# Another order for the list of work in a clustered-attention and SiLU kernel, with some V loads on another queue

## The chip, the cores and the metric

The kernel runs on one core of a Trainium2 chip. Its time is the time of one execution on the device in microseconds (us); lower is better. The program is one launch, and its outputs are float32.

## The reference

Clustered attention is followed by a two-layer block. There are 4 batches, 8 heads, 768 rows, head size 64 and 16 centroids for each head; a query sees only the keys that fall to the same centroid as it does.

```python
q_n, k_n, c_n = (each divided by its norm + 1e-06)
q_assign = argmax(einsum('bhsd,hcd->bhsc', q_n, c_n))      # the same for k
mask = q_assign[:, :, :, None] == k_assign[:, :, None, :]
scores = where(mask, q @ k^T / sqrt(64), -1e9)
attn = exp(scores - max); attn = attn / (sum(attn) + 1e-09)
x = (attn @ v)  -> [3072 tokens, 512]
h = x @ w_in                                               # 512 x 2048
out = (h / (1 + exp(-h))) @ w_out                          # 2048 x 512
```

## The kernel before, in words

The attention has 32 heads ("jobs" 0 to 31, of batches 0 to 3), and each job is 6 scores tiles and 6 exponentials. The block behind it works on a batch in two halves of 384 tokens. Everything on the chip is issued from one string, `order`, a list of 1796 words. A loop at the end takes word after word, splits it at its points and calls the function of that name, so a word's place in the list is the place of its instructions in the in-order queue of every engine that they go to. Buffers and banks are handed out in the same order. The first number of a word is the job or the batch; a last letter names the engine (A ScalarE, D VectorE, P GpSimd, S SyncE), and what follows @ names the bank.

```python
    for word in order:
        word, _, n = word.partition("@")
        name, *rest = word.split(".")
        words[name](tuple(rest), [int(y) for y in n] or None)
    ...
    def load_v(i, eng=nc.sync):
        vn = mp.tile([128, NJ, D], f32, name="vn", bufs=5)
        eng.dma_start(vn.rearrange("p j d -> p (j d)"), v[i // H, i % H].rearrange("(p j) d -> p (j d)", j=NJ))
        vns[i] = vn
```

The words that the rest speaks of, with their lines in the profile:

- `ld.25` loads the queries and keys of job 25 as raw float32 (L108, two DMA issues on SyncE). `hi` (L120 on ScalarE, L124 on VectorE) and `lo` (L129) split them into two float16 parts, and `tp` (L138) transposes these by a DMA on SyncE.
- `L`, `ls`, `mx`, `ge` (L176, L188, L204, L213) work out which centroid each row belongs to. `sc` (L220 and L221, GpSimd) scales the codes; `cx` (L229, a transposing DMA on SyncE, cdt<-od) turns them; `mv` (L233, a DMA, ab<-cdt) puts them beside the transposed keys.
- `v.28.S` loads one job's V, 192 KB, from SyncE; with P at its end it loads it from GpSimd (L289). `vc` casts it on GpSimd (L294).
- `s` (L353) is two of a job's scores matmuls, and `x` (L358) the exponential on ScalarE. `pv` (L370) is the product with V, `nm` (L380, L382) the division by the sum, on VectorE.
- `xd` (L409, xt<-xn) transposes two heads' normalised result by a DMA on SyncE. The tile `xt` of one half of a batch is whole when four of them have landed: `xd.8.1`, `xd.10.1`, `xd.12.1` and `xd.14.1` for the second half of batch 1.
- `q` (L547) are the seven block products of a Quad, by which x @ w_in is done with seven products of half size in place of eight; `tt` (L507) are the sums of blocks of `xt` that they take, on VectorE. Product 1 starts a bank named qa, 6 and 7 add to that bank; product 2 starts qb; product 5 starts qg and 3 adds to it. `qc` copies a bank before it goes on being added to (L557 on ScalarE, L559 on VectorE), `qa` (L564) adds, `qt` (L571) is the tanh, `qg` (L584) the gate. So product 7 of a Quad, which adds to bank qa, can't start until the copy `qc` number 2 has read that bank. Plain units of the same layer are `au`, `t`, `g` (L418, L438, L441).
- `pp`, `p1`, `pa`, `pu`, `pc`, ... (L683 to L718) are the same seven-product scheme for the second layer (`pc` is L708, on VectorE); `b`, `be`, `bs` are plain parts of it (L596, L602 or L604, and the store L609). `tw` (L629) and `un` (L495) are sums of weights, on VectorE.
- `np` is the place where the banks change from pairs to single ones, some 40 us ahead of the end.

Of the kernel before, what the change touches and what calls it, by code (L numbers as in the profile page):

```python
# [34 lines left out]
def kernel(  # L35
# [771 lines left out]
    def stk_ev(pst1):  # L807
# [25 lines left out]
        qa.0.0.1.1 qt.0.0.0.1 s.34 au.0.0.12@2 qg.0.0.0.1 q.0.0.1.6 od.1 qt.0.0.1.0 un.4.1 q.0.0.1.5@3 v.9.S s.32
        qg.0.0.1.0 qc.0.0.1.2.A qa.0.0.0.2 qc.0.0.1.5.A vc.10 q.0.0.1.7 qa.0.0.1.2 q.0.0.1.3 qa.0.0.1.3 x.32 q.0.0.0.4
        qt.0.0.0.3 qg.0.0.0.3 s.31 q.0.0.1.4 t.0.0.12 g.0.0.12 qt.0.0.1.3 qg.0.0.1.3 au.0.0.13@3 lo.8 tp.8 hi.9.D
        hi.10.A t.0.0.13 pv.0.1@1 qt.0.0.1.1 g.0.0.13 b.0.0.0.0@2 b.0.0.0.1 hi.11.A lo.11 x.31 x.34 nm.0.1 qg.0.0.1.1
        tp.11 qt.0.0.0.2 au.0.0.14@0 s.39 x.39 s.35 x.35 b.0.0.0.2 t.0.0.14 g.0.0.14 lo.9 s.37 x.37 v.15.S au.0.0.15@3
        t.0.0.15 tp.9 b.0.0.1.0@1 vc.9 s.38 x.38 s.33 x.33 qt.0.0.1.2 b.0.0.1.1 ld.13 g.0.0.15 lo.10 qg.0.0.0.2 s.45
        x.45 L.8.32@3 ls.8 hi.12.A mx.8 qg.0.0.1.2 s.40 x.40 b.0.0.0.3 be.0.0.0.D lo.12 pv.2.1@3 s.42 x.42 L.11.32@2
        nm.2.1 ls.11 tp.10 ld.14 s.41 b.0.0.1.2 s.36 x.41 s.47 x.47 ge.8 cd.8@2 ce.8.D cg.8 x.36 L.9.32@0 b.0.0.1.3  # L840
        s.46 be.0.0.1.A xp.0.1@2 pv.4.1@3 vc.15 tp.12 od.2 ls.9 mx.9 xe.0.1.A xp.2.1@0 ge.9 v.8.S s.44 hi.13.D lo.13
        x.46 s.43 mx.11 cd.9@2 ce.9.D nm.4.1 xe.2.1.A cg.9 L.10.32@1 b.0.0.2.0@0 b.0.0.2.1 v.11.S ls.10 hi.14.D x.44
# [267 lines left out]
```

## Time and profile before

| what | value |
|---|---|
| time, median of 3 runs | 297.5 us (297.18 to 299.89) |
| the profiled execution | 298.51 us, of which the span of instructions is 296.6 us |
| granted TensorE clock, mean | 0.993 |
| TensorE busy | 285.2 us, 96% of the span |
| VectorE busy | 262.2 us, 88% |
| ScalarE busy | 247.6 us, 83% |
| GpSimd busy | 61.9 us, 21% |

In the rows below PE is TensorE, PEld its loading of weights, DVE VectorE, ACT ScalarE, POOL GpSimd, SP SyncE; SPq and POOLq are the issues of DMAs by these two. A row of a timeline has start, duration, engine, line, operation, what is written and read, and the number of instructions in it; what stands in brackets at its end is how long the engine had waited and for what. A row of a table of windows has the stretch, its length, the busy time of each engine in it with the number of instructions, the granted clock, the DMA share and GB/s.

### The profile page before, as it was taken

The page shows a single profiled execution, that of the slowest core. Times are in us where ns is not written, and L with a number is a line of the kernel's source. Part 1 is how long each engine was busy: PE and PEld are TensorE (multiplying, and loading weights), DVE is VectorE, ACT ScalarE, POOL GpSimd, SP SyncE. Part 2 cuts the span into 40 slices and gives each one's busy share as a digit, 9 for nine tenths or more (in the row PEclk, how much of TensorE's full clock was granted, in tenths as well). Part 3 has the DMA queues.
Part 4 walks back from the last instruction along what each step waited for, and adds up shares of the span by engine and source line. Part 5 has one row for each costly group of instructions (what it writes and reads, how often), then busy time and mean ns, then how long its engine had stood idle before and what let it go on. Part 6 is the DMA issues. An engine that isn't in the chain of part 4 may idle for free.

```text
span 296.6 us, 8938 instructions
## 1 busy us (share of the span) xinstructions
PE 285.2 (96%) x3561; PEld 223.5 (75%) x3561; DVE 262.2 (88%) x578; ACT 247.6 (83%) x431; POOL 61.9 (21%) x116
## 2 busy tenths in 40 slices
PE   7899999999999999999699999999999999899995
PEld 3777757576866668778487887887888889799984
DVE  5998699899999999998889999999998888699863
ACT  5999999986998799999589998789999867947541
POOL 2499310121004122235231031253100000000000
PEclk9999999999999999999899999999999999999999
DMA  6978999997989869998689999654212202201023
GB/s 213 295 208 134 192 222 293 186 188 186 236 204 203 219 163 212 190 165 199 152 212 239 155 276 157 92 132 97 67 27 65 86 0 86 86 2 35 3 105 111
DMA packets 80554, 45.21 MB, mean 152 GB/s; under 512 B 58368, under 2 KB 77120, under 8 KB 80512
## 3 DMA queue, kind: packets, MB, share of 16 engines
q1 hardware_dynamic: 76080, 38.39, 57.2%
q0 software_dynamic: 4000, 5.82, 10.9%
q8 instruction: 28, 0.46, 0.6%
q10 hardware_dynamic: 432, 0.43, 0.4%
q14 instruction: 14, 0.11, 0.1%
HBM read 27.30 MB, written 6.29 MB: 113 GB/s over the span
## 4 chain that ended last, share of the span: by engine, by line
PE 49%; DVE 5%; DMA 1%; issue 1%; ACT 0%; SPq 0%; DVEq 0%
PE po L683 17%; PE pS L353 9%; PE qa L547 7%; PE pO L370 6%; PE ph L418 4%; PE qg L547 3%; PE qb L547 2%; DMA raw<-in_k_dram 1%; PE psN L176 1%; DVE hl L129 1%; DVE gt L584 1%; DVE gt L441 1%; DVE mxn L204 1%; DVE od L213 0%; DVE L L188 0%
## 5 line engine op out<-in xcount | busy, mean ns | idle before, releaser
L358 ACT ACTIVATE P<-pS 128x768 f16<-128x768 f32 x192 | 150.7, 821 | 12.6 <-PE pS L353 9.6
L353 PE MATMUL pS<-ab 128*128 128x384 f16 x384 | 88.3, 326 | 0.3 <-ACT P L358 0.3
L353 PEld LDWEIGHTS <-ab 128*128 128x128 f16 x384 | 33.7, 98 | 11.8 <-issue 1.0
L370 PEld LDWEIGHTS <-P 128*128 128x128 f16 x1152 | 39.8, 97 | 3.4 <-DVE ab L278 0.3
L370 PE MATMUL pO<-vt,P 128*128 128x65 f16 x1152 | 41.5, 193 | 0.2 <-DVE ab L278 0.2
L294 POOL CAST vt<-vn 128x384 f16<-128x384 f32 x32 | 20.8, 661 | 75.8 <-DMA vn<-in_v_dram 64.0
L683 PEld LDWEIGHTS <-gt 128*128 128x128 f16 x328 | 32.2, 99 | 5.8 <-issue 0.6
L547 PEld LDWEIGHTS <-ws 128*128 128x128 f16 x352 | 30.4, 98 | 8.0 <-issue 2.4
L418 PE MATMUL ph<-xt,win_s 128*128 128x384 f16 x160 | 32.2, 326 | 0.3 <-DVE cc L564 0.3
L129 DVE SCALAR_TENSOR_TENSOR hl<-raw,hl 128x768 f16<-128x768 f32 (+3 forms) x35 | 31.4, 902 | 0.9 <-ACT hl L120 0.7
L683 PE MATMUL po<-wout_s,gt 128*128 128x256 f16 x216 | 28.2, 278 | 0.5 <-DVE ot L708 0.5
L571 ACT ACTIVATE tn<-cc 128x384 f32<-128x384 f32 x48 | 24.9, 530 | 4.1 <-DVE cc L564 3.8
L584 DVE SCALAR_TENSOR_TENSOR gt<-tn,cc 128x384 f16<-128x384 f32 x48 | 26.8, 565 | 0.9 <-ACT tn L571 0.8
L547 PEld LDWEIGHTS <-win_s 128*128 128x128 f16 x264 | 23.3, 99 | 5.4 <-issue 1.7
L596 PE MATMUL po<-wout_s,gt 128*128 128x512 f16 x96 | 24.1, 379 | 0.1
L441 DVE SCALAR_TENSOR_TENSOR gt<-tn,ph 128x384 f16<-128x384 f32 x40 | 21.6, 548 | 1.8 <-ACT tn L438 1.7
L418 PEld LDWEIGHTS <-win_s 128*128 128x128 f16 x160 | 15.2, 97 | 9.4 <-issue 0.6
L438 ACT ACTIVATE tn<-ph 128x384 f32<-128x384 f32 x40 | 20.0, 522 | 1.6 <-PE ph L418 0.8
L547 PE MATMUL qa<-tt,ws 128*128 128x192 f16 x176 | 21.1, 249 | 0.0
L176 PEld LDWEIGHTS <-ab 128*128 128x128 f16 x458 | 16.8, 97 | 3.9 <-DVE ab L163 0.6
L382 DVE TENSOR_TENSOR xn<-pO,zr 128x384 f16<-128x384 f32 x32 | 17.8, 558 | 1.1
L176 PE MATMUL psN<-stk,ab 128*128 128x32 f16 (+1 forms) x458 | 18.5, 188 | 0.1
(126 smaller groups left out, 476.0 us busy)
## 6 DMA issues: line engine op xcount, KB each, us to landing
raw<-in_k_dram SPq DMA_DIRECT2D x31, 192.0 KB, 3.6
out_dram<-ot SPq DMA_DIRECT2D x23, 256.0 KB, 2.6
vn<-in_v_dram SPq DMA_DIRECT2D x27, 192.0 KB, 4.0
raw<-in_q_dram SPq DMA_DIRECT2D x24, 192.0 KB, 3.6
win_s<-in_moe_w_in_dram POOLq DMA_DIRECT2D x8, 256.0 KB, 6.6
wout_s<-in_moe_w_out_dram POOLq DMA_DIRECT2D x4, 512.0 KB, 13.6
cp<-gt SPq DMA_DIRECT2D x4, 256.0 KB, 3.9
vn<-in_v_dram POOLq DMA_DIRECT2D x5, 192.0 KB, 3.5
```

The source lines that it names most:

```text
L129: nc.vector.scalar_tensor_tensor(out=hl[:, s, 1, :], in0=raws[job.name][:, s, :], scalar=QS, in1=hl[:, s, 0, :], op0=ALU.mult, op1=ALU.sub ...
L176: nc.tensor.matmul(L[:, n % g, :, n // g], ab[:, i, :], stk[:, job.groups[i // 3][0], x : x + w], start=(x == 0), stop=(x + w == 2 * HC),)
L353: nc.tensor.matmul(pS[:, e, 0:HALF], abs_[kj.name][:, kn, :], rhs, start=True, stop=True)
L358: nc.scalar.activation(out=P, in_=pst.pop(u)[:, :, 0:HALF], func=AF.Exp, bias=0.0, scale=ESC)
L370: nc.tensor.matmul(o[:, (2 * t + h) * VW : (2 * t + h + 1) * VW], Ps[i + h, c, j // 2][:, j % 2, ts(t, 128)], vtb[(i + h) % 13][:, j, 0:VW ...
L418: nc.tensor.matmul(ph[:, 0:HALF], win_s[:, r, ts(fb, 128)], xts[b, c][:, r, :], start=(r == 0), stop=(r == NR - 1))
L441: nc.vector.scalar_tensor_tensor(out=gt[:, fb, :], in0=tn, scalar=1.0, in1=ph[:, 0:HALF], op0=ALU.add, op1=ALU.mult)
L547: nc.tensor.matmul(o[:, g * QT : (g + 1) * QT], w, y, start=(k in (1, 2, 5) and g == 0 and r == 0), stop=(r == 1), skip_group_check=True,)
L571: nc.scalar.activation(out=t, in_=self.src(n), func=AF.Tanh, bias=0.0, scale=1.0)
L584: eng.scalar_tensor_tensor(out=self.gt[:, f : f + 2, h], in0=self.tn[n].rearrange("p (g n) -> p g n", g=2), scalar=1.0, in1=self.src(n).re ...
L596: nc.tensor.matmul(po, gts[b, c][:, fc, ts(t, 128)], wout_s[:, fc, :], start=(fc == 0), stop=(fc == NFB - 1))
L683: nc.tensor.matmul(o, l[:, f, :], x, start=(f == 0 and k in begins), stop=(f == HK - 1), skip_group_check=True)
```

## The change

Only the string `order` changes. The first 245 words, the opening up to about 39 us of the profile, stay. The other 1551 words come in another order. They are the same words but for a few engine letters:

- V loads: `v.9`, `v.12`, `v.14`, `v.19`, `v.20`, `v.23`, `v.24` and `v.31` go from SyncE's queue to GpSimd's, `v.25` and `v.30` the other way (GpSimd issues 11 in place of 5, SyncE 21 in place of 27).
- `mv.17`, `mv.18`, `mv.21`, `mv.26` go from GpSimd's queue to SyncE's.
- The copies `be.0.0.0` and `be.0.1.0` go from VectorE to ScalarE; `hi.10`, `hi.12`, `hi.19` from ScalarE to VectorE; `hi.17`, `hi.27` from VectorE to ScalarE; some 14 of the `qc` copies change between the two, nearly as many each way (ScalarE has 38 in place of 39).

Of the list itself, the first changed line and the one that takes its place:

```diff
-        ld.10 qc.0.0.0.1.A ld.9 s.30 t.0.0.6 q.0.0.0.2@3 s.29 ld.12 ae.0.0.7 t.0.0.7 tt.0.0.1 tt.0.0.2 tt.0.0.4
+        ld.10 qc.0.0.0.1.A v.10.S s.30 ae.0.0.7 tt.0.0.1 tt.0.0.2 tt.0.0.4 q.0.0.0.2@3 t.0.0.6 qa.0.0.0.1 g.0.0.6
...
```

What this does to the queues is shown at three places.

SyncE, the last DMA issues up to the fourth transposition of batch 1's second half (`xd.14.1`, the last row of each piece). Before:

```order
L409 DMA_TRANSPOSE xt<-xn 128x3x128 x2
L138 DMA_TRANSPOSE ab<-hl 128x12x128
L609 DMA out_dram<-ot 128x512
L229 DMA_TRANSPOSE cdt<-od 128x2x128
L289 DMA vn<-in_v_dram 128x384
L409 DMA_TRANSPOSE xt<-xn 128x3x128
L108 DMA raw<-in_q_dram 128x384
L108 DMA raw<-in_k_dram 128x384
L609 DMA out_dram<-ot 128x512
L229 DMA_TRANSPOSE cdt<-od 128x2x128 x2
L409 DMA_TRANSPOSE xt<-xn 128x3x128
```

And now:

```order
L138 DMA_TRANSPOSE ab<-hl 128x12x128 x2
L233 DMA ab<-cdt 16x6x256
L138 DMA_TRANSPOSE ab<-hl 128x12x128
L108 DMA raw<-in_q_dram 128x384
L108 DMA raw<-in_k_dram 128x384
L229 DMA_TRANSPOSE cdt<-od 128x2x128 x2
L409 DMA_TRANSPOSE xt<-xn 128x3x128 x2
L233 DMA ab<-cdt 16x6x256
L229 DMA_TRANSPOSE cdt<-od 128x2x128
L409 DMA_TRANSPOSE xt<-xn 128x3x128
```

From the program's start to that row SyncE issues seven fewer DMAs: four V loads, two stores, the two issues of `ld.25` and one `cx` (of job 21) fewer, and two `mv` (17 and 18) more. `ld.25` now stands right behind the row.

ScalarE in the first Quads (batch 0), from the copy of bank qa of Quad 0.0.1 to the exponential `x.32` and the next rows. Before:

```order
L557 ACTIVATE cc<-qa 128x384
L571 ACTIVATE tn<-cc 128x384 x2
L557 ACTIVATE cc<-qa 128x384
L557 ACTIVATE cc<-qg 128x384
L358 ACTIVATE P<-pS 128x768
L571 ACTIVATE tn<-qa 128x384
```

And now:

```order
L557 ACTIVATE cc<-qa 128x384 x2
L358 ACTIVATE P<-pS 128x768
L571 ACTIVATE tn<-cc 128x384 x2
L557 ACTIVATE cc<-qg 128x384
L557 ACTIVATE cc<-qa 128x384
L358 ACTIVATE P<-pS 128x768
```

The copies 2 (qa) and 5 (qg) of Quad 0.0.1 have changed places; what stands ahead of these two on ScalarE since the opening is the same set of instructions in both.

GpSimd around the scalings of jobs 18 to 21 (each scaling is a row of L220 and one of L221). Before, from `mv.17` and `mv.18`, with the scalings of 19, 20 and 21 and the load `v.26` behind them:

```order
L233 DMA ab<-cdt 16x6x256 x2
L220 TENSOR_SCALAR od<-od 128x2x16x3
L221 TENSOR_SCALAR od<-od 128x2x16x3
L220 TENSOR_SCALAR od<-od 128x2x16x3
L221 TENSOR_SCALAR od<-od 128x2x16x3
L220 TENSOR_SCALAR od<-od 128x2x16x3
L221 TENSOR_SCALAR od<-od 128x2x16x3
L289 DMA vn<-in_v_dram 128x384
```

And now, with the scalings of 18, 19 and 20:

```order
L220 TENSOR_SCALAR od<-od 128x2x16x3
L221 TENSOR_SCALAR od<-od 128x2x16x3
L289 DMA vn<-in_v_dram 128x384
L220 TENSOR_SCALAR od<-od 128x2x16x3
L221 TENSOR_SCALAR od<-od 128x2x16x3
L294 CAST vt_82<-vn 128x6x64
L220 TENSOR_SCALAR od<-od 128x2x16x3
L221 TENSOR_SCALAR od<-od 128x2x16x3
```

The load of `v.22` and its cast (`vc.22`, tile vt_82) now stand between these scalings, so that the scaling of job 20 is behind the cast.

More of the change, by code (lines that the diff above doesn't have):

```diff
@@ L833 @@
[L833 to L842, printed above, removed]
@@ new lines @@
+        s.76 x.76 q.1.0.0.1@0 qc.1.0.0.1.D s.75 x.75 q.1.0.1.2@3 qa.1.0.1.1 tt.1.0.4 tp.20 qt.1.0.1.0 q.1.0.0.2@1
+        qa.1.0.0.1 q.1.0.0.6 qc.1.0.0.2.A qg.1.0.1.0 qt.1.0.0.0 s.78 x.78 q.1.0.0.5@3 hi.21.A s.83 pv.8.1@1
+        qc.1.0.0.5.D q.1.0.0.3 qg.1.0.0.0 x.83 ld.23 q.1.0.1.6 qc.1.0.1.2.A sc.16 cx.16 nm.8.1 q.1.0.0.7 xd.8.1 s.82
+        x.82 qa.1.0.0.3 q.1.0.1.5@1 L.18.32@3 qa.1.0.0.2 qt.1.0.0.2 qc.1.0.1.5.D q.1.0.0.4 qt.1.0.0.3 s.79 x.79 cx.17
+        ls.18 lo.21 s.85 q.1.0.1.3 au.1.0.5@3 x.85 qg.1.0.0.3 qa.1.0.1.3 q.1.0.1.7 hi.22.D t.1.0.5 vc.19 qg.1.0.0.2
@@ new lines @@
+        s.113 x.113 nm.18.0 sc.23 cx.23 q.1.1.1.2@2 qc.1.1.1.1.D qa.1.1.1.1 q.1.1.1.6 vc.25 q.1.1.1.3 s.122
+        qc.1.1.1.2.D qa.1.1.1.3 t.1.1.4 qt.1.1.1.0 g.1.1.4 s.112 x.112 tp.25 qg.1.1.0.0 q.1.1.1.7 qa.1.1.1.2 mv.22.S
+        au.1.1.7@2 t.1.1.7 g.1.1.7 lo.26 kp.1.0 kp.1.1 tp.24 au.1.1.13@1 t.1.1.13 g.1.1.13 pv.20.0@0 x.122 nm.20.0
+        s.116 x.116 qg.1.1.1.0 q.1.1.1.4 qt.1.1.1.3 qg.1.1.1.3 mv.23.P s.118 x.118 ld.28 au.1.1.6@2 vc.26 s.115
+        t.1.1.6 x.115 au.1.1.5@0 t.1.1.5 pe.1.0.p ps.1.1.x.1 au.1.1.15@1 ld.27 s.114 g.1.1.6 x.114 g.1.1.5 ps.1.1.x.2
@@ new lines @@
+        t.2.0.15 mv.31.S q.2.1.0.1@0 qg.2.0.1.1 mv.28.P g.2.0.15 s.150 t.2.0.12 g.2.0.12 qc.2.1.0.1.D x.150 vc.28
+        tt.2.1.1 s.152 x.152 pv.24.0@1 s.156 au.2.0.14@3 x.156 nm.24.0 t.2.0.14 mv.27.P s.153 uu.x.hl2 tt.2.1.2
+        q.2.1.0.2@2 q.2.1.0.6 qg.2.0.1.2 q.2.1.1.1@1 qa.2.1.0.1 x.153 sc.29 cx.29 qc.2.1.0.2.A s.151 tt.2.1.3 sc.30
+        g.2.0.14 q.2.1.0.5@2 qc.2.1.0.5.D qc.2.1.1.1.A x.151 tt.2.1.4 s.155 x.155 q.2.1.0.7 qa.2.1.0.2 qt.2.1.0.2
+        q.2.1.1.2@3 qa.2.1.1.1 qt.2.1.1.0 cx.30 q.2.1.0.3 qa.2.1.0.3 s.158 qg.2.1.1.0 x.158 q.2.1.0.4 q.2.1.1.6 s.154
@@ new lines @@
+        x.154 ps.2.0.p.1 pp.2.0.p.1@3 qt.2.1.0.3 pf.1.1.p qg.2.1.0.2 s.157 qt.2.1.0.1 pv.26.0@2 ps.2.0.p.2 qg.2.1.0.3
+        s.169 x.157 x.169 q.2.1.1.5@0 mv.29.S s.160 x.160 p1.2.0.p qc.2.1.1.2.D q.2.1.1.7 s.161 un.3.2 qc.2.1.1.5.D
+        qa.2.1.1.2 q.2.1.1.3 qa.2.1.1.3 s.159 x.161 x.159 mv.30.P qg.2.1.0.1 pp.2.0.p.6 nm.26.0 qt.2.1.1.2 qg.2.1.1.2
+        s.165 q.2.1.2.1@0 x.165 s.166 x.166 qt.2.1.1.1 v.30.S un.4.2 pe.1.1.p un.1.3 un.2.3 pv.28.0@2 nm.28.0
+        q.2.1.1.4 s.164 qt.2.1.1.3 qg.2.1.1.3 qg.2.1.1.1 x.164 s.163 pp.2.0.p.5 x.163 s.162 q.2.1.2.2@1 s.167
@@ new lines @@
+        qc.2.1.2.1.D kp.2.0 qa.2.1.2.1 q.2.1.2.6 xd.26.0 v.31.P x.162 un.3.3 q.2.1.2.5@2 qc.2.1.2.2.D pf.1.1.x x.167
+        ps.2.0.p.3 un.4.3 s.171 vc.30 vc.31 pv.30.0@1 qt.2.1.0.0 x.171 qt.2.1.2.0 s.168 x.168 xd.28.0 nm.30.0 s.173
+        qc.2.1.2.5.D q.2.1.2.7 q.2.1.3.1@1 qa.2.1.2.2 x.173 s.170 x.170 qc.2.1.3.1.D q.2.1.2.3 qa.2.1.2.3 s.172
+        q.2.1.2.4 x.172 qg.2.1.2.0 q.2.1.3.6 qc.2.1.3.2.D qt.2.1.2.3 qg.2.1.2.3 xd.24.0 pu.2.0.p qg.2.1.0.0 s.174
+        x.174 pv.24.1@2 nm.24.1 s.175 pp.2.0.p.7 pc.2.0.p q.2.1.3.5@0 qc.2.1.3.5.D x.175 s.177 x.177 q.2.1.3.2@2
@@ new lines @@
+        qa.2.1.3.1 qt.2.1.3.0 q.2.1.3.7 q.2.1.3.3 qa.2.1.3.3 s.185 x.185 qa.2.1.3.2 pp.2.0.p.2@2 qg.2.1.3.0
+        pp.2.1.x.1@0 ps.2.0.p.4 s.176 x.176 pa.2.0.p qt.2.1.3.2 s.183 pp.2.0.p.3 kp.2.1 p1.2.1.x ps.2.1.x.1 ps.2.1.x.3
+        ps.2.1.x.2 qt.2.1.2.1 qg.2.1.2.1 qt.2.1.3.1 qg.2.1.3.1 q.3.0.0.1@2 q.2.1.3.4 qt.2.1.3.3 qt.2.1.2.2 s.178
+        qg.2.1.3.3 xd.30.0 x.178 tt.3.0.1 pp.2.0.p.4 qc.3.0.0.1.A pd.2.0.p pe.2.0.p x.183 tt.3.0.2 pp.2.1.x.6
+        pp.2.1.x.5 q.3.0.0.2@3 qa.3.0.0.1 qg.2.1.2.2 q.3.0.0.6 qt.3.0.0.0 tt.3.0.3 qg.3.0.0.0 qg.2.1.3.2 tt.3.0.4
@@ new lines @@
+        x.187 qc.3.0.1.2.A q.3.0.1.3 qa.3.0.1.3 pp.2.1.p.6 x.189 pp.2.1.p.5 pu.2.1.p s.190 qt.3.0.1.0 qg.3.0.1.0
+        q.3.0.3.1@2 s.191 pp.2.1.p.2@1 pa.2.1.p qc.3.0.3.1.A qt.3.0.1.1 qg.3.0.1.1 pp.2.1.p.7 pc.2.1.p q.3.0.1.7
+        xd.28.1 qa.3.0.1.2 pe.2.1.x x.191 x.190 np ps.2.1.p.4 q.3.0.3.6 q.3.0.2.2@4 q.3.0.2.1@6 qc.3.0.2.1.D
+        q.3.0.3.2@1 q.3.0.1.4 qa.3.0.3.1 pv.30.1@7 qa.3.0.2.1 qt.3.0.1.3 qg.3.0.1.3 q.3.0.2.6 qt.3.0.1.2 qc.3.0.3.2.D
+        nm.30.1 q.3.0.3.5@5 qc.3.0.3.5.D q.3.0.2.5@1 qc.3.0.2.2.A qc.3.0.2.5.D qt.3.0.0.2 pp.2.1.p.3 al qz.3.0.3.0
@@ new lines @@
+        q.3.1.2.1@0 qz.3.0.2.0 xp.30.1@4 q.3.0.2.7 qa.3.0.2.2 q.3.0.2.3 qa.3.0.2.3 xe.30.1.A tt.3.1.2 q.3.0.3.7
+        q.3.1.0.1@7 qc.3.1.0.1.D q.3.0.2.4 pp.2.1.p.4 qa.3.0.3.2 q.3.1.0.5@1 qc.3.1.0.5.D qc.3.1.2.1.A qz.3.0.2.3
+        q.3.1.0.6 q.3.0.3.4 qz.3.0.3.3 pd.2.1.p q.3.0.3.3 qa.3.0.3.3 qz.3.0.3.1 tt.3.1.3 q.3.1.2.6 q.3.1.2.2@6
+        qa.3.1.2.1 q.3.1.0.3 qc.3.1.0.2.A ps.3.0.p.1 qz.3.0.2.1 q.3.1.1.1@3 ps.3.0.p.2 qa.3.1.0.3 pf.2.1.p q.3.1.3.1@2
+        tt.3.1.4 qz.3.0.2.2 qc.3.1.3.1.A q.3.1.0.2@5 qa.3.1.0.1 q.3.1.0.7 q.3.1.2.5@4 qc.3.1.2.5.A qc.3.1.1.1.A
@@ new lines @@
+        q.3.1.3.3 qa.3.1.3.3 pp.3.1.x.6 pp.3.1.x.5 qa.3.1.3.2 q.3.1.3.4 qz.3.1.3.2 qz.3.1.1.1 q.3.1.1.7 qa.3.1.1.2
+        qz.3.1.2.3 pp.3.0.p.3 qz.3.1.3.3 pp.3.0.p.4 ps.3.1.x.3 pu.3.1.x pd.3.0.p q.3.1.1.4 pp.3.1.x.7 pc.3.1.x
+        qz.3.1.1.3 pp.3.1.x.2@5 qz.3.1.2.1 qz.3.1.3.1 pp.3.1.p.1@2 ps.3.1.x.4 qz.3.1.1.2 qz.3.1.0.2 ps.3.1.p.1
+        ps.3.1.p.2 ps.3.1.p.3 pe.3.0.p pp.3.1.p.2@1 p1.3.1.p pp.3.1.p.5@7 pp.3.1.p.6 pp.3.1.x.4 pa.3.1.x p5.3.1.p
+        pf.3.1.x ps.3.1.p.4 pp.3.1.x.3 pd.3.1.x pe.3.1.x pa.3.1.p pu.3.1.p pp.3.1.p.7 pc.3.1.p pp.3.1.p.3 pf.3.1.p
@@ L954 @@
+        pp.3.1.p.4 pl.3.1.p pz.3.1.p py.3.1.p pm.3.1.p
     """.split()
```

192 lines of the change are left out of this document (78 added, 114 removed).

## The prediction

> **What bounds the kernel now.** I read the page's busy shares first, then the stretches of the span, then who waited for whom, then the queues around the one place that stands out.
>
> ```profile
> PE 285.2 (96%) x3561; PEld 223.5 (75%) x3561; DVE 262.2 (88%) x578; ACT 247.6 (83%) x431; POOL 61.9 (21%) x116
> ```
>
> TensorE is busy for 96% of the span, VectorE for 88%. Both lists give TensorE the same instructions, so another order can only win what TensorE loses in waits or in clock. Where it loses, a table of stretches shows (the first difference of the lists stands at about 38.6 us).
>
> ```profile
> core 0: us, PE busy (x) PEld busy (x) DVE busy (x) ACT busy (x) POOL busy (x), PEclk, DMA share, GB/s
> 40.00:48.00 8.00, 7.28 (x61) 4.91 (x59) 8.00 (x21) 7.53 (x17) 0.00 (x0) 1.00 1.19 247
> 38.60:142.80 104.20, 103.34 (x1252) 73.56 (x1250) 97.14 (x205) 95.32 (x166) 19.66 (x38) 1.00 0.97 205
> 142.80:147.60 4.80, 2.25 (x16) 1.56 (x15) 4.73 (x11) 1.71 (x4) 2.11 (x4) 0.81 0.48 111
> 146.00:149.00 3.00, 2.60 (x14) 2.06 (x14) 2.98 (x8) 0.52 (x1) 1.11 (x2) 0.50 0.93 180
> 147.60:257.00 109.40, 109.40 (x1379) 90.50 (x1377) 100.94 (x217) 97.29 (x169) 17.03 (x35) 0.99 0.56 117
> 257.00:259.00 2.00, 1.10 (x12) 0.81 (x10) 1.37 (x4) 1.69 (x3) 0.00 (x0) 1.00 0.50 172
> 259.00:293.30 34.30, 34.26 (x380) 31.89 (x377) 27.38 (x55) 17.49 (x41) 0.00 (x0) 1.00 0.13 45
> ```
>
> From 38.6 us on TensorE is idle for 0.86 us before 142.8 (0.72 of it in 40 to 48), 2.55 us in the next 4.8, never up to 257, 0.90 us in 257 to 259 and 0.04 after that. The clock granted falls once, to 0.50, right behind the longest pause. So there is one hole worth filling, at 143 to 149, and about 1.8 us in all elsewhere. The table of waits and TensorE's own timeline name what it waited for:
>
> ```profile
> PE qg L547 <- DMA xt<-xn: 2.1, 1, 2.1
> PE qa L547 <- ACT P L358: 0.9, 1, 0.9
> ...
> 145.19 0.41 PE L547 MATMUL qg<-xt,ws 128*128 128x192 f16 x3 [2.07 <-DMA xt<-xn]
> 146.40 1.87 PE L683 MATMUL po<-wout_s,gt 128*128 128x256 f16 x8 [0.47 <-DVE ot L708]
> ...
> 148.27 1.18 PE qa L547 x8
> 149.45 0.33 PE pS L353 x2
> 149.78 0.87 PE po L683 x8
> 150.98 0.33 PE qa L547 x4
> ```
>
> The first two rows are the table's totals by releaser, the next two TensorE's own timeline, the last four the chain that ended last. Product 3 of Quad 1.1.0 waited 2.07 us for the transposition `xd.14.1`, the pair's products then 0.47 us for VectorE. Behind that, at half clock, eight `po` took 1.87 us where 0.87 is what they take at 149.78 (+1.00), and eight `qa` 1.18 where four take 0.33 at 150.98 (+0.52). **The hole costs 2.07 + 0.47 + 1.00 + 0.52 = 4.06 us.**
>
> On the page "TensorE: Matmul & The Clock Gate" of the Trainium skill (section "Part 1: The HAM clock gate (the "warmup" mystery)") the clock falls only after an idle window of about 3.4 us. The rows speak against so long a window here, with 0.50 behind pauses of 2.07 and 0.47 us; by the page alone the two pauses would be worth their 2.54 us, the slow clock would have another cause, and the sum would be 1.5 us higher.
>
> **What made the transposition late.** SyncE's queue:
>
> ```profile
> 98.08 1.49 SPq L138 DMA_TRANSPOSE ab<-hl  x1
> 119.28 0.36 SPq L289 DMA_DIRECT2D vn<-in_v_dram  x1
> 128.28 2.88 SPq L409 DMA_TRANSPOSE xt<-xn  x2
> 133.92 0.57 SPq L609 DMA_DIRECT2D out_dram<-ot  x1
> 135.84 0.58 SPq L289 DMA_DIRECT2D vn<-in_v_dram  x1
> 137.74 0.59 SPq L108 DMA_DIRECT2D raw<-in_q_dram  x1
> 138.37 0.43 SPq L108 DMA_DIRECT2D raw<-in_k_dram  x1
> 139.44 2.52 SPq L229 DMA_TRANSPOSE cdt<-od  x2
> 142.06 1.99 SPq L409 DMA_TRANSPOSE xt<-xn  x1
> 149.66 0.60 SPq L233 DMA_DIRECT2D ab<-cdt  x1
> ...
> DMA to landing us min/median/max: 2.3/3.3/4.5
> ...
> 142.29 0.56 DVE L124 TENSOR_SCALAR hl<-raw 128x768 f16<-128x768 f32 x1 [2.54 <-DMA raw<-in_k_dram]
> ```
>
> From 98.08 us on, issue follows issue with gaps of up to 0.1 us (139.44 + 2.52 to 142.06), so the queue itself is what `xd.14.1` waits in: it is issued at 142.06 and lands 3.1 us later, about the median of the landing row (that of `xt`, 98 to 150 us). TensorE could have used it at 145.19 - 2.07 = 143.12. The last row is VectorE: it stood 2.54 us at `hi.25`, waiting for the load that SyncE had issued at 138.37, and that is why `pc` came 0.47 us late.
>
> **The change part by part.** *SyncE's queue.* Seven fewer issues stand ahead of `xd.14.1`. What goes in the unbroken stretch, each with its gap, is `v.28` at 119.28 (0.46), the store at 133.92 (0.67), `v.24` at 135.84 (0.67), `ld.25` at 137.74 and 138.37 (1.11) and one of the two `cx` that reach from 139.44 to 142.06 (1.31): 4.2 us. What comes in is `v.27` (as 135.84, 0.6) and two `mv` (as 149.66, 0.65 each): 1.9 us. Net 2.3 us. The other three V loads and the other store that go, less two V loads that come, were issued ahead of 98 us; they would add up to some 2.1 us if the queue was as full there, and nothing if it wasn't. So the transposition is issued **2.3 to 4.4 us earlier**. The reader moves too: in the new list eight `po` (0.87), four `pS` (0.65) and four `qa` (0.33) that stood ahead of it on TensorE now stand behind it, 1.85 us. To leave no wait, the landing must come 2.07 + 1.85 - 0.5 = 3.4 us earlier; the 0.5 is that the new reader is a product that takes a VectorE sum of `xt` (two `tt`) only in part behind other work. The wait that stays is therefore 0 to 1.1 us, and I take the middle, **0.5 us**, with no fall of the clock, since the pause at 257 to 259 (0.90 us) has 1.00 beside it.
>
> The two `mv` are new waits on SyncE: `mv.18` needs the landing of `cx.18`, and `cx.20` and `xd.14.1` are queued behind it. Between `cx.18` and it stand `cx.19` and two `xd`: 2.6 + 3.0 = 5.6 us from the start of `cx.18` by the rows at 139.44 and 128.28. A `cdt` lands like an `xt`, 4.5 us at most, so it costs only its issue. `mv.17` likewise has two `tp`, a store and a load behind its `cx`.
>
> *VectorE at that place.* `ld.25` now follows `xd.14.1`, so it comes later than before; but `hi.25` stands nine instructions behind the `tt` that wait for that transposition. Their landing is 3.1 us behind the issue of `xd.14.1`; the load's keys are issued some 1.3 + 0.6 us behind the same issue and land 3.8 us later (138.37 to 142.2), thus 2.6 us behind the `tt`'s start. By VectorE's rows
>
> ```profile
> 143.77 0.69 DVE L664 TENSOR_TENSOR gt<-gt,sg 128x1024 f16<-128x1024 f16 x1
> 144.59 0.56 DVE L382 TENSOR_TENSOR xn<-pO,zr 128x384 f16<-128x384 f32 x1
> 145.93 0.42 DVE L708 TENSOR_TENSOR ot<-po,uu 128x256 f32<-128x256 f32 x1
> 146.80 0.55 DVE L564 TENSOR_TENSOR cc<-qb,cc 128x384 f32<-128x384 f32 x1
> ```
>
> four of the nine take 2.2 us, so with the other five the load is there first. The 0.47 us goes. If the load were slower by a transposition (1.3 us), the cover would still nearly reach.
>
> *The opening of the rewritten part, 40 to 48 us.* Here ScalarE is the engine waited for: 7.53 of 8 us busy, and VectorE 8.00.
>
> ```profile
> 46.78 0.49 ACT L557 ACTIVATE cc<-qa 128x384 f32<-128x384 f32 x1
> 47.17 0.48 ACT L557 ACTIVATE cc<-qg 128x384 f32<-128x384 f32 x1
> 47.32 0.49 PE L547 MATMUL qa<-tt,ws 128*128 128x192 f16 x4
> ```
>
> Product 7 of Quad 0.0.1 starts at 47.32, as soon as copy 2 (46.78 + 0.49) has read its bank; copy 5 follows. In the new list copy 5 goes first, and the set of instructions ahead of the two on ScalarE is the same, so product 7 waits one copy longer: **+0.5 us** (0.48). Bounds: nothing, if the 0.72 us of idle time here close up, to 1.0 if VectorE's additions come late as well.
>
> *What I cost at nothing.* The other moved V loads are transfers of the same size; a load from GpSimd holds POOL, 21% busy, and a load off SyncE shortens a queue nobody else waits for. The swapped copies and `hi` leave ScalarE and VectorE as they were to within 0.5 us of 248 and 262, and up to 257 us neither holds TensorE; without that cover each swapped copy would cost 0.5. At the bank switch (257 to 259) TensorE waits 0.90 us for an exponential; the new list also has two exponentials right ahead of `np`, so no change, within 0.9 either way. The end has 0.04 us idle in 34 and the same work.
>
> **The sum.** -4.06 + 0.5 + 0.5 = -3.06 us on the profiled execution's 298.51 (1.9 of it outside the span, unchanged): 295.45. The median of the runs is 1.0 us under that execution, so **294.4 us**.
>
> **The rivals.**
> *The cleaner case*: the wait is gone entirely, the opening's idle time absorbs the copy, some of the 0.90 us goes: -4.06 to -5.0, 292.5 to 293.4. For it: the early part of SyncE's queue is also shorter.
> *Small waits elsewhere*: 1551 words stand anew, with VectorE at 93% (97.14 of 104.20) and ScalarE at 91% in the first stretch; each exponential or copy that a bank now waits for costs a few tenths. Two to four of these are 1 to 2.5 us: 295.5 to 297.
> *The slow clock is not the pause's doing* and comes again without it: -2.54 + 1.0 gives 296.0. That the clock falls nowhere else behind 38.6 us speaks against it. It is what the TensorE page's window of 3.4 us would make of these rows.
> *The hole stays*: only 2.3 us saved on SyncE and a landing of 4.5 us (the slowest in the row) in place of 3.1. The wait is 3.4 - 2.3 + 1.4 = 2.5 us, and the clock falls with it: 2.5 + 1.5 + 0.5 - 4.06 = +0.4 at worst, 297 to 298.
> *A load on GpSimd holds the transposition up* (the slower side). The scaling of job 20 now stands behind the cast of `v.22`, which waits for that load's landing; `cx.20` on SyncE waits for the scaling, and `xd.14.1` is the next issue.
>
> ```profile
> vn<-in_v_dram POOLq DMA_DIRECT2D x5, 192.0 KB, 3.5
> win_s<-in_moe_w_in_dram POOLq DMA_DIRECT2D x8, 256.0 KB, 6.6
> wout_s<-in_moe_w_out_dram POOLq DMA_DIRECT2D x4, 512.0 KB, 13.6
> ```
>
> From the load's issue to the scaled code are 3.5 us of landing and about 1.6 of cast and scaling, 5.1; SyncE meanwhile issues `cx.18`, `cx.19`, two `xd` and `mv.18`, 2.6 + 3.0 + 0.65 = 6.3. So 1.2 us are spare. Landing like the other loads on that queue, 6.6 us, the scaling is 1.9 late, which ends with the case before; like the slowest, 13.6, it is 8.9 late: 0.5 + 8.9 + 1.5 - 4.06 + 0.5 = +7.3, about 305. It makes the kernel slower by over 1% from a landing of some 9.2 us on. Against it: the five V loads on that queue landed in 3.5 us in the middle.
> The page "SBUF — State Buffer" of the Trainium skill has a trap of this kind (a passage named the "DVE blocks DMA" trap): a DMA issued from GpSimd can't get its descriptors written while VectorE holds the port that the two share. No row here shows such a delay for these loads, though VectorE was busy beside them.
>
> **How the numbers follow.** Chances: forecast 0.36, cleaner 0.22, small waits 0.14, a slow clock of its own 0.05, the hole stays 0.13, GpSimd 0.10. A measurement of this kernel can tell about 1% from no change: 294.5 and 300.5. The forecast's own spread, 293.6 to 295.3, has a little over half below 294.5: faster 0.22 + 0.22 = 0.44; same 0.14 + 0.14 + 0.05 + 0.13 = 0.46; slower 0.10. The range leaves out the GpSimd case and the far ends: 292.3 to 298.4.
>
> **What would show it.** Right: at Quad 1.1.0, some 140 to 146 us, no wait of TensorE over 1 us, no granted clock of 0.50, `xd.14.1` issued at 138 to 140; product 7 of Quad 0.0.1 some 0.5 us later than 47.3, behind two copies on ScalarE; 257 to 259 alike. Wrong: a wait for `xt` over 1.5 us, a wait of SyncE at `cx.20` for POOL, new waits of TensorE for ScalarE or VectorE in 48 to 140 us.

## The result: 294.98 us in place of 297.5

The changed kernel takes 294.98 us in the median of nine runs (294.51 to 296.03) against 297.5 (296.93 to 299.89): a ratio of 0.9908, 95% interval 0.9883 to 0.9934. Run again on another chip, it gave 294.56 against 297.81 there, 0.9905 (0.987 to 0.994). Two executions at a clock of about 0.6, 416.59 us of before and 485.75 us of one version below, are left out of the ratios and the counts. The profiled execution took 294.78 us, its span 292.9, 3.7 less than in the profile of before. Of that, 1.5 is TensorE busy for less time, and the rest, 2.2, is less idle time of TensorE:

```profile
PE 283.7 (97%) x3561; PEld 222.8 (76%) x3561; DVE 260.1 (89%) x579; ACT 246.8 (84%) x430; POOL 62.9 (21%) x118
```

Stretches around the places that were read in before (their ends are near the same work, not at the same instruction) show the hole at Quad 1.1.0 closed, and in these stretches no clock below 1.00:

```profile
core 0: us, PE busy (x) PEld busy (x) DVE busy (x) ACT busy (x) POOL busy (x), PEclk, DMA share, GB/s
38.60:48.00 9.40, 8.50 (x73) 6.12 (x71) 9.23 (x24) 9.25 (x19) 0.00 (x0) 1.00 1.19 239
48.00:138.00 90.00, 89.26 (x1110) 62.95 (x1108) 83.94 (x177) 80.35 (x139) 20.97 (x39) 1.00 1.03 203
138.00:146.00 8.00, 8.00 (x99) 6.67 (x97) 7.69 (x20) 7.05 (x12) 3.17 (x8) 1.00 0.71 166
146.00:253.00 107.00, 106.84 (x1355) 87.92 (x1353) 98.90 (x212) 94.69 (x162) 15.84 (x33) 1.00 0.55 123
253.00:256.00 3.00, 3.00 (x41) 2.87 (x40) 2.99 (x7) 1.43 (x3) 0.00 (x0) 1.00 0.23 87
256.00:289.60 33.60, 33.45 (x368) 31.11 (x364) 26.86 (x55) 20.01 (x46) 0.00 (x0) 1.00 0.13 45
```

TensorE's waits over 0.25 us behind 38.6 us are down to three, from its timeline:

```profile
40.81 0.81 PE L418 MATMUL ph<-xt,win_s 128*128 128x384 f16 x4 [0.39 <-DVE cc L564]
47.40 0.49 PE L547 MATMUL qa<-tt,ws 128*128 128x192 f16 x4 [0.39 <-ACT cc L557]
55.28 0.48 PE L353 MATMUL pS<-ab 128*128 128x384 f16 x2 [0.65 <-ACT P L358]
```

The second is the product 7 of the prediction. The third is new. SyncE's queue issues `xd.14.1` (here behind `cx.20`, with `ld.25` behind it) at 137.97, 4.1 us earlier than before:

```profile
135.99 0.60 SPq L233 DMA_DIRECT2D ab<-cdt  x1
136.69 1.19 SPq L229 DMA_TRANSPOSE cdt<-od  x1
137.97 1.21 SPq L409 DMA_TRANSPOSE xt<-xn  x1
139.23 0.58 SPq L108 DMA_DIRECT2D raw<-in_q_dram  x1
139.87 0.41 SPq L108 DMA_DIRECT2D raw<-in_k_dram  x1
```

Openings differ by chance: the first Quad product began at 38.5 to 40.4 us in the fourteen profiles of this study, with the same list up to there. So below, kernels are also compared by TensorE's time from that product to its last end, worked out from the traces: 254.8 us in the profile of before and 250.8 in that of the changed kernel, 3.9 apart.

### The profile page after: what moved, and what is told of

It is laid out like the page before. It is cut to its first block, busy times and chain, and to the rows that moved or that the text cites. A ratio compares the mean times of both kernels' runs of the same rounds, so it can differ in the third digit from the quotient of the medians.

```text
span 292.9 us, 8949 instructions
## 1 busy us (share of the span) xinstructions
PE 283.7 (97%) x3561; PEld 222.8 (76%) x3561; DVE 260.1 (89%) x579; ACT 246.8 (84%) x430; POOL 62.9 (21%) x118
## 4 chain that ended last, share of the span: by engine, by line
PE 72%; DMA 9%; DVE 7%; ACT 7%; SPq 2%; issue 2%; ACTq 0%; DVEq 0%
PE po L683 18%; PE pS L353 16%; PE pO L370 10%; PE qa L547 8%; DMA raw<-in_k_dram 8%; PE ph L418 6%; PE qg L547 4%; PE po L596 4%; ACT P L358 3%; PE psN L176 2%; PE qb L547 2%; DVE hl L129 2%; SPq L108 1%; DMA raw<-in_q_dram 1%; ACT hl L120 1%
## 5 line engine op out<-in xcount | busy, mean ns | idle before, releaser
L294 POOL CAST vt<-vn 128x384 f16<-128x384 f32 x32 | 21.4, 681 | 73.8 <-PE pO L370 39.5
L683 PE MATMUL po<-wout_s,gt 128*128 128x256 f16 x216 | 27.5, 273 | 0.0
L220 POOL TENSOR_SCALAR od<-od 128x96 f16<-128x96 f16 x16 | 8.7, 547 | 47.2 <-DVE od L213 47.1
```

What stands on the lines that cost most here:

```text
L683: nc.tensor.matmul(o, l[:, f, :], x, start=(f == 0 and k in begins), stop=(f == HK - 1), skip_group_check=True)
```

## The experiments

The words moved are given as a diff of the list.

**The hole opened again in the changed kernel.**

```diff
- xd.14.1 ... ld.25 ... sc.21 cx.21 ... v.25.S
+ ld.25 sc.21 cx.21 v.25.S xd.14.1 ...
```

> The list of the changed kernel with its SyncE queue made worse at the one place: ld.25, cx.21 (with its scaling sc.21) and the load v.25 stand ahead of xd.14.1 again. VectorE's order stays. Theory: xd.14.1 is issued 1.11 + 1.31 + 0.5 = 2.9 us later than the 137.97 of the changed kernel, lands about 144, and TensorE waits about 2 us at the product that reads xt (it started at 141.81 without a wait); if the pause is what lowers the clock, the granted clock falls behind it and the whole is +2 to +3.7 us, 297 to 298.7. Rival A (the gain is spread over the list): within 1 us of the changed kernel, 294 to 296. Rival B (clock not the pause's doing): +2 us at a clock of 1.00.

Measured: 298.79 us against 298.23 of before on that chip, ratio 1.0019 (0.9984 to 1.0055). None of the lead is left.

```profile
145.43 0.41 PE L547 MATMUL qb<-xt,win_s 128*128 128x192 f16 x3 [2.94 <-DMA xt<-xn]
```

The pause is longer than the 2 us expected (the transposition is issued at 141.28 and takes 2.61 us to issue). From the first Quad product TensorE takes 254.5 us. The clock was 1.00 in the profile, but under 0.997 in 8 of the 12 executions. So the order of these few DMAs is enough to lose the lead, and rival A, by which this kernel would have stayed within 1 us of the changed one, falls. That the whole lead is the hole's is not shown by it: the reopened pause of 2.94 us is longer than the 1.3 to 2.1 us in three profiles of before (below), and the four executions with a full clock have a median of 297.3 us, 0.9 under before's.

**Is closing it enough? The hole closed in the kernel before.** Three versions.

```diff
- ld.25 bs.0.1.1 ... cx.21 ... hi.24.A hi.25.D lo.25 ... xd.14.1 ... ge.23
+ bs.0.1.1 ... hi.24.A ... xd.14.1 ld.25 cx.21 ... ge.23 hi.25.D lo.25
```

> The list of before with four words moved and nothing else: ld.25 and cx.21 now stand right behind xd.14.1 (SyncE issues that transposition 2.4 us earlier: 1.11 for the two load issues, 1.31 for the transposing DMA), and hi.25, lo.25 stand behind ge.23, so that VectorE doesn't wait for the later load. TensorE's and ScalarE's order is that of before. Theory (SyncE's queue ahead of xd.14.1 is the whole gain): TensorE's wait for xt falls from 2.07 to under 0.3 us, the 0.47 us wait for pc goes, the granted clock stays at 1.00, and the time is that of the changed kernel or a little under it, 293.5 to 295 us. Rival A (the gain is spread over the new list): at most a third of it, 296.5 to 297.5. Rival B (the slow clock is not the pause's doing): the wait goes and the clock still falls to 0.5 near 146 us, 295 to 296.5.

Measured: 301.53 us against 298.23, ratio 1.0092 (1.0056 to 1.0128): slower. The wait for `xt` was gone, but a longer one stood 8 us behind it:

```profile
117.53 0.82 PE L547 MATMUL qa<-tt,ws 128*128 128x192 f16 x8 [1.42 <-ACT cc L557]
153.18 0.82 PE L353 MATMUL pS<-ab 128*128 128x384 f16 x2 [4.33 <-DMA ab<-cdt]
...
147.80 1.09 POOL L233 DMA_DIRECT2D ab<-cdt  x2 [6.34 <-DMA cdt<-od]
```

The last row is GpSimd: it stood 6.34 us for the turned codes of job 21, which `cx.21` now issued later, and `mv.20`, which job 20's scores needed, stood behind `mv.21` in its queue. I had moved a DMA past what waits for it on another in-order queue. The 1.42 us at 117.53, ahead of the edit, is of another kind: ScalarE waited 1.55 us there for a load, which it did not in the first profile of the same order.

```diff
- mv.21.P ... mv.20.P
+ mv.20.P mv.21.P
```

> The list of before with ld.25 and cx.21 behind xd.14.1 and hi.25, lo.25 behind ge.23, as in the first run, and in addition mv.21 behind mv.20 on GpSimd's queue, so that mv.20 (job 20, whose scores waited 4.33 us) does not stand behind the transposition of job 21. Theory (SyncE's queue ahead of xd.14.1 is nearly the whole gain): no wait over 0.5 us in 140 to 160 us, TensorE from the first Quad product to its end takes about 252 us (254.8 in before, 250.8 in the changed kernel, 0.9 of whose lead is the wait at 257 to 259, which stays here), time 294.5 to 296.5 us. Rival (the changed kernel's lead comes from the whole of its list): 297 to 298.5 us, as before.

Measured: 298.16 us against 297.81, ratio 1.0011 (0.9983 to 1.0038): no gain, as the rival has it. The wait for `xt` and the 4.33 us are gone, and VectorE is late instead:

```profile
149.75 1.27 PE L370 MATMUL pO<-vt,P 128*128 128x65 f16 x36 [1.36 <-DVE ot L715]
...
147.24 0.86 DVE L124 TENSOR_SCALAR hl<-raw 128x768 f16<-128x768 f32 x1
148.13 0.96 DVE L129 SCALAR_TENSOR_TENSOR hl<-raw,hl 128x768 f16<-128x768 f32 x1
149.00 0.68 DVE L715 TENSOR_TENSOR ot<-po,uu 128x512 f32<-128x512 f32 x1
```

`hi.25` and `lo.25`, 1.8 us that stood in the hole, now stand ahead of the addition (L715) that the next product with V waits for.

```diff
- ge.23 hi.25.D lo.25 ... nm.18.0
+ ge.23 ... nm.18.0 hi.25.D lo.25
```

> As the fifth run (before, with ld.25, cx.21 behind xd.14.1 and mv.21 behind mv.20), but with hi.25 and lo.25 behind the division of job 18 (nm.18.0) in place of ahead of pd, where their 1.8 us of VectorE made TensorE wait 1.36 us for L715. Theory (closing the hole moves 1.8 us of VectorE work out of it into a stretch in which VectorE is full, and what the hole gives is given back where that work lands): the 1.36 us wait goes, TensorE from the first Quad product to its end takes about 252 us (253.4 in the fifth run), time 296.3 to 297.3 us, against 298.2 of the fifth run. Rival (VectorE and ScalarE hold the stretch wherever the 1.8 us stand): the wait comes again at another instruction between 148 and 160 us, 297.5 to 298.5.

Measured: 298.06 us against 297.75, ratio 1.0013 (0.9986 to 1.004). The waits moved as the rival says, though they got smaller:

```profile
144.11 0.41 PE L547 MATMUL qg<-xt,ws 128*128 128x192 f16 x3 [0.27 <-DMA xt<-xn]
153.26 0.49 PE L547 MATMUL qa<-tt,ws 128*128 128x192 f16 x4 [0.66 <-DVE cc L559]
154.08 0.48 PE L353 MATMUL pS<-ab 128*128 128x384 f16 x2 [0.32 <-ACT P L358]
```

TensorE takes 252.5 us in this profile, which is less than before's, but the time does not show it. So none of the three versions gains by closing the hole. In the last two profiles TensorE waits for VectorE within the next 10 us instead, in the first of them behind the very work that had stood in the hole. That no place in the list of before would do, and which part of the new list makes room for that work, no run shows.

**What the hole is worth in other executions of before.** Two more profiles of the same kernel.

> The kernel before itself, for a second profile: the first one had the earliest start of the first Quad product (38.50 us; the others 38.6 to 40.4) and a clock of 0.993, while nearly all other executions of this list show 0.998 to 1.000. Theory A (SyncE's queue sets when xd.14.1 lands, so TensorE's wait there takes in whatever TensorE is late by then): with a later start of the Quads the wait for xt is shorter, 0.5 to 1.8 us, the clock stays at 1.00, and TensorE from the first Quad product to its end takes 252.5 to 253.5 us. Theory B (the first profile is typical): a wait of 2 us again. Theory C (this list also loses time in places that differ from execution to execution, as the 1.42 us for a ScalarE copy at 117.53 in the first run): waits over 0.4 us between 48 and 140 us that the first profile doesn't have.

> The same, for a third profile, with the same expectations as e11_before_again: a wait for xt that is the shorter the later the Quads began (A), 2 us again (B), or waits over 0.4 us between 48 and 140 us that differ from profile to profile (C).

Measured: 298.12 and 298.36 us. The waits at the hole, one profile after the other:

```profile
145.23 0.41 PE L547 MATMUL qg<-xt,ws 128*128 128x192 f16 x3 [1.31 <-DMA xt<-xn]
146.28 1.03 PE L683 MATMUL po<-wout_s,gt 128*128 128x256 f16 x8 [0.31 <-DVE ot L708]
147.66 0.51 PE L547 MATMUL qa<-tt,ws 128*128 128x192 f16 x4 [0.34 <-DVE tt L507]
```

```profile
145.89 0.41 PE L547 MATMUL qg<-xt,ws 128*128 128x192 f16 x3 [1.57 <-DMA xt<-xn]
```

The Quads began 0.9 and 0.7 us later than in the first profile, and TensorE stood 0.8 and 1.2 us behind it ahead of the hole. The product that reads the tile started at 145.23 and 145.89 against 145.19, so the wait was 1.31 and 1.57 in place of 2.07. Theory A holds: TensorE's lateness shortens the wait, since the landing does not move with it (in the third profile it came 0.7 later, behind an issue of 2.60 us in place of 1.99). The clock stayed at 0.999 and 1.000, and TensorE took 253.2 and 253.7 us from the first Quad product (252.5 to 253.5 were expected), 1.0 to 1.5 less than in the first profile. Theory C is seen only as 0.17 us at 116.31.

**The bank switch.** In the kernel before TensorE waited 0.90 us at 257 to 259; in the changed one it does not.

```diff
- q.3.0.3.1@2 qc.3.0.3.1.A ... x.186 ... qc.3.0.3.5.D s.189 x.189 np
+ q.3.0.3.1@2 s.189 ... x.186 x.189 qc.3.0.3.1.A ... qc.3.0.3.5.D np
```

> As e9_before_hole_closed, and at the bank switch the scores s.189 stand three pieces of work earlier on TensorE and their exponential ahead of a copy on ScalarE. Theory (the 0.90 us wait at 257 to 259, which the changed kernel doesn't have, is the second part of its lead): the wait falls to 0.1 to 0.3 us, -0.6 to -0.8 us against the kernel beside it; with both parts closed TensorE's stretch is 251.2 to 251.5 us and the time 295.5 to 296.5. Rival: the wait only moves to another exponential or copy near it, the same time as the kernel beside it.

Measured: 298.17 us against 298.06 of the kernel beside it and 297.75 of before, ratio to before 1.0006 (0.9977 to 1.0035). In the profile the 0.90 us is gone and the stretch is 252.0 us, 0.5 shorter than beside it (0.24 us came again as a wait for an exponential just ahead); the timed runs don't show that much. Why the two kernels with shorter profiles than before take as long as it in the runs is open: both profiled executions (297.08 and 296.85 us) were among the faster third of their kernel's, so they may leave out waits that others have.

**The queue of the V loads alone, both ways.**

```diff
- v.9.P v.12.P v.14.P v.19.P v.20.P v.23.P v.24.P v.31.P v.25.S v.30.S
+ v.9.S v.12.S v.14.S v.19.S v.20.S v.23.S v.24.S v.31.S v.25.P v.30.P
```

This is the edit of the changed kernel; in the list of before it is the reverse.

> The list of the changed kernel, every word in its place, but each V load on the queue that it had before (9, 12, 14, 19, 20, 23, 24, 31 on SyncE, 25 and 30 on GpSimd). Theory: ahead of xd.14.1 SyncE has six more issues, of which v.23 certainly lies in the full stretch: the transposition is 0.5 to 3 us later, with about 0.3 us to spare, so TensorE waits 0.2 to 2.7 us for xt; time +0.2 to +3 us, 295.2 to 298. Rival (the letters of the V loads don't matter, only the order of the rest): within 0.3 us of the changed kernel. Rival (GpSimd's loads cost the changed kernel time): faster than it, 293.5 to 294.5.

> The list of before, every word in its place, but each V load on the queue that the changed kernel gives it. Theory: v.24 (0.67 us) leaves the full stretch of SyncE's queue ahead of xd.14.1, and v.9, v.12, v.14, v.19 and v.20 leave it earlier on: the wait of 2.07 us for xt shrinks to between 0 and 1.4 us, while VectorE's wait at hi.25 and the 0.47 us stay less the same shift; time 294.5 to 297. Rival (GpSimd's own queue takes it back, since the loads stand ahead of scalings and casts there): no gain or a loss, 297.5 to 300.

Measured: the list of the changed kernel with the old queues 295.3 us against 298.23, ratio 0.9897 (0.9859 to 0.9934), as good as with the new ones; the list of before with the new queues 298.62, ratio 0.9991 (0.9963 to 1.0019). The queue of these loads is worth nothing that the runs can tell, and the theory's 0.2 to 3 us for the first and its gain for the second did not come. In the first, SyncE issued `xd.14.1` 3.4 us later than in the changed kernel, nearly as late as in before:

```profile
141.32 1.22 SPq L409 DMA_TRANSPOSE xt<-xn  x1
144.72 0.49 PE L547 MATMUL qb<-xt,win_s 128*128 128x192 f16 x4
```

But TensorE came to the product that reads the tile 2.9 us later itself (144.72 against 141.81), after waits of 0.83 us at 55 and 0.88 us at 80 among others, and did not wait. This was the slowest execution of that kernel, at 296.9 us; whether the faster ones waited there, one profile can't say. So a late issue alone is no hole: it is the lead of TensorE over the landing that counts. In the second, `xd.14.1` was issued at 141.77, only 0.3 us earlier than in before; TensorE was 1.8 us later than in before ahead of the hole, and waited there for other things:

```profile
143.44 0.50 PE L353 MATMUL pS<-ab 128*128 128x384 f16 x2 [0.54 <-DMA ab<-cdt]
146.56 1.03 PE L683 MATMUL po<-wout_s,gt 128*128 128x256 f16 x8 [0.23 <-DVE ot L708]
148.07 0.51 PE L547 MATMUL qa<-tt,ws 128*128 128x192 f16 x4 [0.48 <-DVE tt L507]
```

**The clock and the length of a pause.**

> As the second run (ld.25, cx.21 and v.25 ahead of xd.14.1 in the changed kernel's list), with ld.26 ahead as well, 1.1 us more on SyncE: a pause of about 4 us in place of 2.94. Theory on the clock (it falls when the pause fills enough of a window that runs freely, so a longer pause lowers it in more executions): a mean clock under 0.996 in at least 10 of 12 executions, where the pause of 2.94 us gave 8 of 12; time +1.1 us for the pause and up to +0.6 for the clock on the 298.8 of that run, 299.5 to 301. Rival (the clock falls from something else): the share stays 8 of 12 or falls.

Measured: 300.32 us against 297.81, ratio 1.0091 (1.0055 to 1.0127), a mean clock under 0.997 in 6 of 6 executions. The pause, and stretches of 3.41 us, the first of which ends where the clock falls:

```profile
146.53 0.64 PE L547 MATMUL qb<-xt,win_s 128*128 128x192 f16 x3 [3.86 <-DMA xt<-xn]
...
142.17:145.59 3.42, 0.50 (x4) 0.23 (x3) 0.00 (x0) 1.80 (x4) 0.00 (x0) 1.00 0.61 182
145.59:149.00 3.41, 2.47 (x14) 1.88 (x14) 1.72 (x6) 0.52 (x1) 0.71 (x2) 0.50 0.31 97
149.00:152.41 3.41, 3.41 (x18) 2.31 (x16) 2.84 (x7) 1.69 (x3) 1.48 (x3) 0.50 0.16 34
```

With 4.33 us (the first version of before above) it was 9 of 9, with 2.94 us 8 of 12, and of before's executions (1.3 to 2.1 us in three profiles) 3 of 26, 0 of 18 and 0 of 22 on three chips. The longer the pause, the more often the clock falls.

**The changed kernel again, and with its two small waits taken out.**

```diff
- qc.0.0.1.5.A qc.0.0.1.2.A ... hi.9.D tp.8 hi.10.D hi.11.A ... nm.0.1 lo.10
+ qc.0.0.1.2.A qc.0.0.1.5.A ... tp.8 hi.11.A ... nm.0.1 hi.9.D hi.10.D lo.10
```

> The changed kernel itself, for a second profile and for times on the same chip as the runs beside it. If its lead is the hole's, TensorE again waits nowhere over 0.7 us behind 38.6 us and the clock of nearly all executions is 0.998 or more: 294.5 to 295.5 us. If the first profile was lucky at the transposition xd.14.1 (about 0.3 us to spare), this one shows a wait for xt of 0.3 to 1.5 us.

> The changed kernel with two moves: copy 2 of Quad 0.0.1 again ahead of its copy 5 on ScalarE, and hi.9, hi.10 on VectorE behind the division of head 0's second half in place of ahead of a gate (VectorE stood 1.44 us there for a load, a tanh waited for the gate, TensorE 0.65 us for an exponential). Theory: the waits of 0.39 us at 47.40 and 0.65 us at 55.28 go, -0.5 to -1.0 us against the changed kernel: 293.8 to 294.6 us. Rival (the work that follows is held by the same ScalarE and VectorE, both over 90% busy here, so the waits turn up a few us later): within 0.3 us of it.

Measured: 294.56 and 294.23 us against 297.81, ratios 0.9905 (0.987 to 0.994) and 0.9887 (0.9856 to 0.9917). In the second profile of the changed kernel nothing waits for `xt` either, so the first was not luck; its stretch is 251.5 us, with two waits that the first profile does not have (0.47 us at 106 for a gate, 0.45 us at 153 for a division). With the moves the 0.39 us becomes 0 at that product (0.3 us come one product later, for an addition), the 0.65 us at the exponential goes, and the stretch is 250.1 us. That the small moves help is seen in the profile; in the runs 0.3 us lie inside both intervals. The kernel with the moves has the lowest median here, and at 0.9887 it is ahead of before.

## Why the prediction was right, and where it was not

The forecast was 294.4 us, a sum of -3.06; the medians lie 2.5 apart (3.25 on the second chip).

- **The hole, -4.06: the place and the cause were right, the size holds for the one execution that it was read from.** On profiled against profiled it is what went: 2.07, 0.47 and the half clock. In ordinary executions of before it is smaller. The second profile has 1.31 + 0.31 + 0.34 = 1.96 us there, the third 1.57, both without a fall of the clock. The term of the sum that was mis-sized is the slow clock (1.52): a mean of 0.993 stood in the first profile, while 63 of 66 executions of before on three chips had 0.997 or more. The prediction also took 1.0 us off the profile's 298.51 to come to the median; the slow clock may be part of that 1.0, and would then be counted twice.
- **SyncE's queue, 2.3 to 4.4 us earlier:** 4.1 us, near the upper end. So the residual wait of 0.5 us did not come: +0.5 too much. Two readings under it were loose: of the other V loads, five go and two come, so that the 2.1 us stand for three, and the gaps between issues reach 0.16 us.
- **VectorE at `hi.25`:** no wait stands there, as argued. But the versions of before showed that this was half of the matter: 1.8 us of VectorE work had lain in the hole, and none of them gained with that work moved elsewhere. The prediction saw that the work moves and asked only whether the load is there in time; it put the place where the 1.8 us land at nothing.
- **The opening, +0.5:** product 7 waits 0.39 us behind two copies, as forecast. But the 0.39 us that before had at another product (`cc` L564, 44.62) went, so the product starts at 47.40, hardly later than 47.32, and 38.6 to 48 us has 0.90 us idle in place of 0.72: +0.2.
- **At nothing, and not nothing:** the change is wider than it was costed. 18 of the `qc` copies change their engine, not some 14 (ScalarE has 37), and 100 words name another bank, which the account of the change leaves out. No run takes these apart. At 257 to 259 the 0.90 us went, which the prediction had held to stay; and +0.65 us came at 55.28. VectorE stood there for a load:

```profile
52.48 1.03 DVE L124 TENSOR_SCALAR hl<-raw 128x768 f16<-128x768 f32 x2 [1.44 <-DMA raw<-in_k_dram]
...
54.00 0.52 ACT L571 ACTIVATE tn<-cc 128x384 f32<-128x384 f32 x1 [1.14 <-DVE gt L584]
```

The gate behind `hi.9` and `hi.10` was late, the tanh on ScalarE behind it, and the exponential behind that. This is the rival of small waits elsewhere; it was there once, and the 0.90 us set it off.

By the profiled pair, then, -4.06 + 0.2 + 0.65 - 0.90 = -4.1, near the 3.9 us measured. With the hole of the second and third profile, -1.96 or -1.57 in place of -4.06, it is -2.0 or -1.6, against 2.5 and 3.25 by the medians: what the rest is stays open. The forecast of -3.06 lies between, and that is in part luck: the 0.5 us of wait that did not come, the opening at 0.2 in place of 0.5, and the 0.90 less the 0.65 us offset half of what the hole was taken too large.

**The GpSimd rival** did not come:

```profile
128.04 0.60 POOL L289 DMA_DIRECT2D vn<-in_v_dram  x1
...
132.63 0.50 POOL L294 CAST vt<-vn 128x384 f16<-128x384 f32 x1 [3.23 <-DMA vn<-in_v_dram]
134.54 0.86 POOL L220 TENSOR_SCALAR od<-od 128x96 f16<-128x96 f16 x1 [1.41 <-DVE od L213]
```

The load of `v.22` landed about 4.6 us after its issue, the cast followed, and then GpSimd stood another 1.41 us for VectorE ahead of job 20's scaling. A landing 1.4 us later would have cost nothing, and SyncE came to `cx.20` only at 136.69, another 1.1 us behind the end of the scaling (135.34 + 0.29). The eleven loads of V from GpSimd landed in 3.6, 4.5 and 7.2 us (least, median, most), longer than the five of before (3.1, 3.5, 4.3); one of 7.2 at this place would have held GpSimd for some 1.2 us and SyncE for about 0.1. What made the first version of before slower is of the same kind, GpSimd's queue standing for a landing, there for 6.34 us.

**The clock rule** (Trainium skill, "TensorE: Matmul & The Clock Gate", section "Part 1: The HAM clock gate (the "warmup" mystery)"): the page has the clock fall after an idle window of about 3.4 us, and calls the window free-running. The pauses of 3.86 and 4.33 us, which always lowered the clock, agree with that. The pause of 2.94 us, which lowered it in two executions of three, and that of 2.07 us in the first profile do not, since neither fills such a window. The half clock of the first profile lasts from 145.80 to 149.22, so it began 0.13 us ahead of the pause of 0.47 us (145.93 to 146.40), and the prediction was wrong to put it behind both pauses. Where a pause lies seems to matter. The half clocks last 3.41 us or twice that, so each trace was cut into stretches of 3.413 us, counted back from the change of its clock near its end; the earlier falls, in three traces, lie on the same cut. The first two rows are from the first profile of before; the third is from the run with 2.94 us, whose clock stayed at 1.00 there. The last two are the ends of the first V queue run and of the second profile of the changed kernel; behind the former the clock fell, behind the latter it did not:

```profile
142.39:145.80 3.41, 1.34 (x12) 0.95 (x11) 3.34 (x6) 1.91 (x4) 0.94 (x2) 1.00 0.31 70
145.80:149.22 3.42, 2.94 (x18) 2.27 (x16) 3.18 (x8) 0.74 (x2) 1.26 (x3) 0.50 0.92 188
...
143.53:146.95 3.42, 1.52 (x16) 1.42 (x16) 1.54 (x5) 0.26 (x1) 0.20 (x1) 1.00 0.58 146
...
290.56:293.97 3.41, 1.38 (x13) 0.98 (x11) 0.57 (x2) 0.38 (x1) 0.00 (x0) 1.00 0.66 231
...
289.81:293.22 3.41, 1.49 (x14) 1.09 (x12) 0.69 (x2) 0.38 (x1) 0.00 (x0) 1.00 0.66 231
```

In the fourteen profiles, behind 45 us, the clock fell at the end of every whole stretch with at most 1.38 us of TensorE work (1.34 here, 0.50 in the run with 3.86 us, 0.00 in that with 4.33), and of none with 1.49 or more. So the stretch need not be idle as a whole: some 2.0 us of idle time inside one were enough, and a longer pause that straddled two of them passed. By an estimate from these rows, a pause of 2.94 us has 2.0 us inside one stretch in (3.41 - 2.94 + 2 x 0.94) / 3.41 = 0.69 of its positions, near the 8 of 12; one of 1.3 or 1.6 us never has, near the 3 of 66. The prediction was right to take the row there, and wrong to take it for the usual case: its pause happened to lie inside one stretch.

## What to carry to other kernels

A wait that one queue sets takes in all the lateness of the engine that waits, so its size in one profile is not what closing it gives: take a second profile, and see what other engines do inside the hole, because that work has to go somewhere. A move on one in-order queue is checked on every queue that waits for it (here `mv.20` behind `mv.21`, 4.33 us). And a half clock in one profile is a term of that execution, not of the kernel, until the clocks of the other executions say the same.
